# Batch 0's keys and queries loaded in turn by head pair, and 2 KB rows for the keys and queries of batches 2 and 3

## The chip, the cores and the metric

The kernel runs on one core of a Trainium2 chip. The metric is the device time of one execution in microseconds (us), lower is better. The core has a matrix engine (TensorE, PE in the profile, with its weight loads as PEld), a vector engine (VectorE, DVE), an activation engine (ScalarE, ACT), a general engine (GpSimd, POOL) and a sync engine (SyncE, SP) which issues transfers. Each engine works through its own queue in order. Matrix results go to PSUM, everything else lies in SBUF, both of 128 partitions.

## The reference

```python
batch, n_heads, seq, head_dim = (4, 8, 768, 64)      # q, k, v
block, window = (32, 16)
k_sum = k.reshape(B, H, nb, block, D).max(axis=3)    # nb = 24 blocks
v_sum = v.reshape(B, H, nb, block, D).mean(axis=3)
scores_l = scale * q @ k.T, kept where abs(i - j) < window
scores_s = scale * q @ k_sum.T + log(block)
a = softmax(concat(scores_l, scores_s))
attn = a @ concat(v, v_sum)
x = attn as [3072 tokens, 512]
h = x @ w_in                                          # [512, 2048]
out = (h * sigmoid(beta * h)) @ w_out                 # [2048, 512]
```

So each query attends to the keys less than 16 places away and to 24 block summaries (maximum of the keys, mean of the values), and the result goes through two products with a gated activation between them.

## The kernel before

The four batches run one after the other. A batch has eight heads, held as four pairs g = 0 to 3: the 64 dimensions of one head in partitions 0 to 63, of the other in 64 to 127. Queries are cut in 12 tiles of 64 (QT). For a tile the 96 keys of its window and the 24 block keys make up to 120 rows of a score tile; a score group is half of a pair's tiles (u = 0 or 1). An exp on ACT (`weigh`, L316) turns a group into weights `e`, and PE multiplies them with the values `ve` (for even tiles) and `vo` (the same values shifted by 64 rows, for odd tiles).

**The head** (L111 to L614) computes attention of batch 0 while its inputs arrive. Everything there is in an order written by hand, and each engine's queue follows it. `sw_load` (L84, issued by POOL) loads rows of 8 consecutive tokens, 2 KB of f32 to a packet, and casts them to bf16 in `krow` and `qrow`; it loads four pairs of keys in four transfers (L122 to L147), then queries 0, 1, and 2 and 3 together (L163 to L165). `turned` (L248) lets PE turn such rows into PSUM, 16 matmuls for a pair; `kt0` (L259) copies the keys to `kT` and may take their block maximum `km` (`key_max_nat`), and `qt_pe` (L272) copies the queries to `qn`. `scores0` (L282) makes a score group straight from `kT`, `km` and `qn`, with masks as extra matmuls (`off`, `edge`). `vm0` averages the values into `vm_one`, `av_split` weighs the values for u = 0, `norm` divides by the sum, `x_pe` turns the result into `xT`. `blank_run` issues matmuls on zeros that nothing uses. The matmuls `begin` (L602) start the first product with `w_in`.

The loads that follow in POOL's queue are four parts of `w_in` (`load_w_in`; the first waits on an exp by `behind`, L578), `w_out` in four parts, and between them `krow` and `qrow` of batch 1 as one transfer each (`more_loads`, L629). SP loads the values: batch 0's pairs 1 to 3 wait until the first query load has landed (L167), batch 1's until the last part of `w_out` has (L639). Batch 1's keys and queries are turned on PE as batch 0's are (`kt_pe`, `qt_pe`).

**Batches 2 and 3** take another way. `hw_load` (L87, issued by SP) loads a pair as 128-row blocks of f32, 256 bytes to a packet, into a staging tile; POOL casts it (`kq_cast`, L453) into a tile of the pool `nat`; a transposing DMA (`kq_dma`, L465) writes `kT` and `qn`; DVE copies the windows of 96 keys (`windows_nat`, L225) and takes the block maximum. This happens while PE runs the first product of the batch before (`h_tile`, L490). The second product (`o_atom`, L513) is interleaved with the scores of the next batch (`scores`, L302), whose moving operand is `q_tile` (L279), 64 consecutive elements of `qn`.

`run` (L530) puts the work of such a stage in order: a list of main steps, and side steps with a position among them, sorted.

Of the kernel before, what the change touches and what calls it, by code (L numbers as in the profile page):

```python
# [11 lines left out]
def kernel(  # L12
# [29 lines left out]
    G = H // 2  # L42
    NK = QT + 2 * W
    CS = (8, 8)
    scale = 1.0 / math.sqrt(D)
    log_block = math.log(block)
    d_model = moe_w_in.shape[0]
# [6 lines left out]

    const = ctx.enter_context(tc.tile_pool(name="consts", bufs=1))
    stage = ctx.enter_context(tc.tile_pool(name="stage", bufs=4))
    natp = ctx.enter_context(tc.tile_pool(name="nat", bufs=4))
    ep = ctx.enter_context(tc.tile_pool(name="ep", bufs=8))
    xp = ctx.enter_context(tc.tile_pool(name="xp", bufs=4))
    op = ctx.enter_context(tc.tile_pool(name="op", bufs=3))  # L60
# [7 lines left out]
    def pair(a, b, g):  # L68
        return a[b, 2 * g:2 * g + 2]
# [14 lines left out]
    def sw_load(t, src, b, lo, hi):  # L84
        return nc.gpsimd.dma_start(out=row_view(t, b, lo, hi), in_=src[b, lo:hi].rearrange("h (p c) d -> p h (c d)", c=CS[b]))

    def hw_load(nm, src, b, g):  # L87
        f = stage.tile([P, 2, J6, D], f32, name=nm + "st", tag=nm + "st")
        stg[(nm, b, g)] = f
        nc.sync.dma_start(out=f[:], in_=pair(src, b, g).rearrange("h (j p) d -> p h j d", p=P))  # L90

    vst = [const.tile([P, JV, D], f32, name=f"vst{g}") for g in range(G)]

# [28 lines left out]
    sw_load(krow, k, 0, 0, 2)  # L122
    identity = const.tile([P, P], bf16, name="identity")
    make_identity(nc, identity)
    sw_load(krow, k, 0, 2, 4)
    band = const.tile([P, QT], bf16, name="band")
    mask = const.tile([P, NT, QT], bf16, name="mask")
    off = const.tile([P, NK + QT], bf16, name="off")
# [14 lines left out]
    nc.vector.memset(A, 0.0)  # L143
    As = A[:, :, 0:nb]
    nc.vector.memset(As, 1.0 / block)
    sw_load(krow, k, 0, 4, 6)
    sw_load(krow, k, 0, 6, 8)  # L147
    select(off[:], -1, [[1, NK + QT]], -1, NEG)
    select(off[:], 2 * W - 1, [[-1, NK + QT]], 1, NEG)
    identity32 = const.tile([P, P], f32, name="identity32")  # L150
# [9 lines left out]
    nc.vector.memset(vm_one[NK:NK + nb, :, :, D:VW], 1.0)  # L160
    for t in (ve, vo):
        nc.vector.memset(t[:, :, :, D:VW], 1.0)
    ql = sw_load(qrow, q, 0, 0, 2)  # L163
    sw_load(qrow, q, 0, 2, 4)
    qe = sw_load(qrow, q, 0, 4, 8)  # L165
    vl = [None] + [load_v0(g) for g in range(1, G)]
    behind(vl[1], ql)  # L167
    select(band[:], -1, [[-1, QT]], 1)
    select(band[:], 2 * W - 1, [[1, QT]], -1)
    select(As, -W, [[P, J6 + 1], [-block, nb]], 1)  # L170
    select(As, block - 1 + W, [[-P, J6 + 1], [block, nb]], -1)

    def more_masks():
        nc.vector.tensor_copy(out=mask[:], in_=band[:, None, :].to_broadcast([P, NT, QT]))
        nc.vector.memset(mask[0:W, 0], 0.0)
        nc.vector.memset(mask[NK:NK + nb], 1.0)

    def clear_kw():
        for g in range(G):
# [36 lines left out]
    def windows_perm(cp, g, src, C):  # L216
# [4 lines left out]
        e = kw[g][:, 0, W:NK]  # L221
        cp(strided(e, [[(NT - 1) * P - W, 2], [C, F + FW], [1, C]]),
           strided(src[:, :, 0:1], [[R - F - FW, 2], [1, F + FW], [cs, C]]))

    def windows_nat(cp, g):  # L225
        cp(kw[g][:, :, 0:NK], strided(kT[g][:, 0:1], [[QT, NT], [1, NK]]))

    def key_max_win(g):
        nc.vector.tensor_reduce(out=km[g][:, NK:NK + nb].rearrange("p (m n) -> p m n", n=2),  # L229
# [46 lines left out]

    et = {}

    def q_tile(g, h, m):  # L279
        return qn[g][h * D:(h + 1) * D, m * QT:(m + 1) * QT]  # L280

    def scores0(g, u, bg, pe=True):  # L282
        s = big[bg]
# [18 lines left out]
    def scores(b, g, u, bg):  # L302
        s = big[bg]
        for j in range(HT):
            m = u * HT + j
            for h in range(2):
                nc.tensor.matmul(s[:, h, j * QT:(j + 1) * QT], kw[g][h * D:(h + 1) * D, m, :], q_tile(g, h, m),  # L307
                                 start=True, stop=True)
        weigh(b, g, u, s)
        if g < G - 1 or b == 1:  # L310
            mask_e(b, g, u)
# [136 lines left out]
                                    in_=xn[(b, g)].rearrange("p j h d -> p (j h d)"))  # L448


    nat = {}

    def kq_cast(eng, nm, b, g):  # L453
        t = natp.tile([P, J6, 2, D], bf16, name=nm + "n", tag=nm + "n")
        nat[(nm, b, g)] = t
        return eng.tensor_copy(out=t[:], in_=stg[(nm, b, g)].rearrange("p h j d -> p j h d"))  # L456

    last_mask = {}

    def key_cast(n, g):  # L460
        i = kq_cast(nc.gpsimd, "k", n, g)
        if g == 0 and n - 1 in last_mask:
            behind(i, last_mask[n - 1])

    def kq_dma(nm, b, g):  # L465
        t = kT[g][:, W:W + S] if nm == "k" else qn[g][:]
        nc.sync.dma_start_transpose(out=t.rearrange("p (j t) -> p j t", j=J6),
                                    in_=nat[(nm, b, g)].rearrange("p j h d -> p (j h d)"))


    def h_begin(i, t, lo, hi):
# [70 lines left out]

    blank_run(30)
    load_beta()
    blank_run(32, QT)
    kt0(0, 0, act_cp)
    more_masks()
    blank_run(12, QT)
    kt0(1, 1, act_cp, False)
    blank_run(8)  # L550
    kt0(2, 2, dve_cp, False)
    key_max_nat(1)
    blank_run(10)
    kt0(3, 0, act_cp, False)
    blank_run(4)
    v_cast(nc.gpsimd, 0)
    v_odd(nc.gpsimd, 0, 0, 3)
    v_odd(nc.gpsimd, 0, 3, 6)
    select(mask[0:NK, NT - 1], QT + W - 1, [[0, QT]], -1)

    def av0(g, t):
        av_split(g, t[:, 0])
        norm(0, g, t, [0])

    qt_pe(0, 0, 1, act_cp)
    vm0(0, one[0], dve_cp)
    blank_run(9)
    vm_rest(nc.gpsimd, 0)
    qt_pe(0, 1, 2, dve_cp)
    scores0(0, 0, 0)  # L570
    scores0(1, 0, 1)
    key_max_nat(2)
    key_max_nat(3)
    we = scores0(0, 1, 2)
    av0(0, one[1])
    scores0(1, 1, 0)
    qt_pe(0, 2, 1, dve_cp)
    behind(load_w_in(0, 512), we)  # L578
    v_cast(nc.gpsimd, 1)
    x_pe(0, 0, 0, dve_cp, one[0])  # L580
    qt_pe(0, 3, 2, act_cp)
    scores0(2, 0, 0)
    v_odd(nc.gpsimd, 1, 0, 3)
    v_cast(nc.vector, 2)
    v_odd(nc.vector, 2, 0, 3)
    scores0(3, 0, 1)
    scores0(2, 1, 2, False)
    vm0s(1, 2, one[1], dve_cp)
    scores0(3, 1, 0, False)
    load_w_in(512, 1024)  # L590
    v_cast(nc.gpsimd, 3)
    av0(1, one[0])
    av_two(0, 1, [big[2][:, 0:1]])
    v_odd(nc.gpsimd, 3, 0, 3)
    vm0(3, big[1][:, 1:2], dve_cp)
    av0(2, one[1])
    x_pe(0, 1, 0, act_cp, one[0])
    av0(3, big[1][:, 0:1])
    load_w_in(1024, 1536)
    load_w_in(1536, 2048)  # L600

# [1 line left out]
        for i in (2 * p, 2 * p + 1):  # L603
            h_begin(i, big[(2, 0, 1)[p % 3]][:, i % 2], lo, hi)

    begin(0, 0, 1)
    begin(1, 0, 1)
    x_pe(0, 2, 0, act_cp, one[1])
    silu_table()
    begin(0, 1, 2)  # L610
    begin(1, 1, 2)
    x_pe(0, 3, 0, dve_cp, one[0])
    begin(0, 2, 3)
    begin(1, 2, 3)  # L614
# [45 lines left out]

    def load_keys(n):
        for g in range(G):
            hw_load("k", k, n, g)


    def scores_at(b, s, pos):
# [41 lines left out]
    for b in range(1, B):  # L708
        n = b + 1
        s = []  # L710
        if n < B:
            for g in range(2):
                s.append((0 + .1 * g, lambda g=g, n=n: hw_load("q", q, n, g)))
            for g in range(G):
                s.append((.5 + g, lambda g=g: key_cast(n, g)))
                s.append((.6 + g, lambda g=g: kq_dma("k", n, g)))
                s.append((3.5 + g, lambda g=g: windows_nat(dve_cp, g)))
                s.append((3.6 + g, lambda g=g: key_max_nat(g)))
                s.append((4.7 + g, lambda g=g: kq_cast(nc.gpsimd, "q", n, g)))
                s.append((8 + g, lambda g=g: key_sums(nc.gpsimd, g)))  # L720
                s.append((6.6 + 1.5 * g, lambda g=g: kq_dma("q", n, g)))
                s.append((12.6 + 1.2 * g, lambda g=g: v_cast(nc.gpsimd, g)))
                s.append((12.7 + 1.2 * g, lambda g=g: v_odd_dma(g)))
            for g in range(2):
                s.append((.7 + g, lambda g=g, n=n: hw_load("q", q, n, g + 2)))
                s.append((2.7 + g, lambda g=g: load_v(n, g)))
                s.append((6.7 + 1.5 * g, lambda g=g: load_v(n, g + 2)))
        if n + 1 < B:
            for g in range(G):
                s.append(((16.31, 16.32, 19.3, 19.31)[g], lambda g=g, n=n: hw_load("k", k, n + 1, g)))  # L730
        late = [x for x in s if x[0] >= 16]
        run([lambda i=i: h_tile(i) for i in range(k2)], [x for x in s if x[0] < 16])
        s = [((x[0] - 16) * 1.2, x[1]) for x in late]
        if n < B:
            scores_at(n, s, [1, 5.9, 8, 10.1])
            av_at(n, s, [10.2, 13.1, 13.2, 13.3], [0, 1, 2, 0])
            for g in range(G):
                s.append(((10.3, 13.35, 13.4, 13.5)[g], lambda g=g: x_dma(n, g)))
            s.append((5.99, lambda: vm_all(big[0], VMC)))
            s.append((6.3, lambda: spread(0)))  # L740
            s.append((8.3, lambda: spread(1)))
        main = [lambda ms=ms, a=a: o_atom(b, ms, a) for ms in range(J6 - (n == B)) for a in range(4)]
        run(main, s)
        if n == B:
            ms = J6 - 1
            for lo, hi in ((0, 256), (256, 512)):
                t = one[0 if lo else 1][:, 0]
                for kk in range(k2):
                    o_mm(ms, kk, t, lo, hi)
                o = op.tile([P, hi - lo], f32, name="o_half", tag=f"o_half{lo}", bufs=1)  # L750
                nc.vector.tensor_copy(out=o[:], in_=t[:, 0:hi - lo])
                nc.sync.dma_start(out=out_r[b * J6 + ms][:, lo:hi], in_=o[:])
# [29 lines left out]
```

## Time and profile before

| | |
|---|---|
| median of three runs | 216.02 us (215.3 to 217.65) |
| the profiled execution | 217.07 us, its span 215.33 us |
| PE clock granted in the span | 1.00 |
| HBM read, written | 27.37 MB, 6.29 MB |
| DMA packets | 85,287, of which 73,728 under 512 B |

A line of the chain of waits gives start, length and what ran; the chain is followed back from the last instruction to whatever released it. A row of the lines' view gives source line, engine, operation, output<-input with shapes, count, then busy time in us and mean ns of one, then idle time of the engine before them and what ended it. In the windows' view each row is a stretch of the span with the busy time of PE, PEld, DVE, ACT and POOL, the granted clock, the DMA share and GB/s. Rows of the timeline give start, length, engine, line, operation, and in brackets the idle time ahead.

Where the time lies: 0 to 25 us is the head; to 50 us the first product of batch 0 (with the last part of its attention in it); to 78 us its second product and batch 1's attention; then 46 us for each of batches 1 and 2 with the attention of the next one, and 45 us for batch 3.

### The profile page before, as it was taken

The page shows a single profiled execution, that of the slowest core. Times are in us where ns is not written, and L with a number is a line of the kernel's source. Part 1 is how long each engine was busy: PE and PEld are TensorE (multiplying, and loading weights), DVE is VectorE, ACT ScalarE, POOL GpSimd, SP SyncE. Part 2 cuts the span into 40 slices and gives each one's busy share as a digit, 9 for nine tenths or more (in the row PEclk, how much of TensorE's full clock was granted, in tenths as well). Part 3 has the DMA queues.
Part 4 walks back from the last instruction along what each step waited for, and adds up shares of the span by engine and source line. Part 5 has one row for each costly group of instructions (what it writes and reads, how often), then busy time and mean ns, then how long its engine had stood idle before and what let it go on. Part 6 is the DMA issues. An engine that isn't in the chain of part 4 may idle for free.

```text
span 215.3 us, 5346 instructions
## 1 busy us (share of the span) xinstructions
PE 207.2 (96%) x2242; PEld 121.0 (56%) x2242; DVE 99.1 (46%) x233; ACT 107.7 (50%) x143; POOL 57.5 (27%) x91
## 2 busy tenths in 40 slices
PE   7789999999999999999999999999999999999993
PEld 7567756665546445665455455654564556654452
DVE  5567766597786612530599212422796200002121
ACT  2258595777676007776681046676660077650000
POOL 7946990010517403441105004433000000000000
PEclk9999999999999999999999999999999999999999
DMA  6999999999949999999699979999527400001212
GB/s 118 181 212 161 191 175 198 206 209 191 225 114 226 269 199 236 230 195 159 147 215 214 247 184 227 180 200 196 136 70 182 120 24 0 0 3 49 97 49 97
DMA packets 85287, 34.09 MB, mean 158 GB/s; under 512 B 73728, under 2 KB 82320, under 8 KB 85264
## 3 DMA queue, kind: packets, MB, share of 16 engines
q1 hardware_dynamic: 68192, 24.05, 55.3%
q0 software_dynamic: 7440, 7.34, 21.3%
q10 hardware_dynamic: 9632, 2.37, 7.6%
q8 instruction: 17, 0.28, 0.6%
q14 instruction: 6, 0.05, 0.1%
HBM read 27.37 MB, written 6.29 MB: 156 GB/s over the span
## 4 chain that ended last, share of the span: by engine, by line
PE 87%; DMA 6%; DVE 3%; issue 1%; ACT 0%; POOL 0%; POOLq 0%; DVEq 0%
PE one L505 36%; PE big L487 29%; PE big L473 5%; PE one L479 3%; DMA xT<-xn 3%; DMA krow<-in_k_dram 3%; PE big L256 3%; PE big L307 3%; PE big L395 2%; PE big L479 2%; DVE xn L422 1%; DVE qn L243 1%; PE big L294 1%; PE big L286 1%; PE big L369 1%
## 5 line engine op out<-in xcount | busy, mean ns | idle before, releaser
L505 PE MATMUL one<-w_out_sb,h_sb 128*128 128x512 bf16 (+1 forms) x400 | 86.3, 371 | 0.0
L500 ACT ACTIVATE h_sb<-big,beta_sb 128x768 bf16<-128x768 f32 x48 | 42.7, 901 | 52.5 <-PE big L487 52.5
L487 PE MATMUL big<-xT,w_in_sb 128*128 128x384 bf16 x384 | 63.0, 326 | 0.3 <-DMA xT<-xn 0.3
L505 PEld LDWEIGHTS <-h_sb 128*128 128x128 bf16 x400 | 37.8, 98 | 40.9 <-issue 0.2
L487 PEld LDWEIGHTS <-w_in_sb 128*128 128x128 bf16 x384 | 37.6, 98 | 25.6 <-issue 0.5
L243 DVE COPY o_sb<-one 128x512 f32<-128x512 f32 x20 | 13.8, 688 | 47.4 <-PE one L505 47.3
L316 ACT ACTIVATE e<-big,bias 128x768 bf16<-128x768 f32 x32 | 27.1, 899 | 7.5 <-PE big L307 4.9
L320 DVE TENSOR_TENSOR e<-e,mask 128x768 bf16<-128x768 bf16 x24 | 14.2, 618 | 19.0 <-ACT e L316 18.9
L325 POOL CAST ve<-vst 128x832 bf16<-128x832 f32 x15 | 13.2, 889 | 9.8 <-DMA vst<-in_v_dram 9.7
L243 DVE COPY kw<-kT 128x1152 bf16<-128x1152 bf16 x8 | 4.0, 496 | 22.5 <-DMA kT<-kn 22.5
L456 POOL CAST qn<-qst 128x768 bf16<-128x768 f32 x8 | 6.6, 830 | 28.7 <-DMA qst<-in_q_dram 28.7
L237 POOL COPY kw<-km 128x288 bf16<-128x288 bf16 x12 | 5.5, 471 | 27.6 <-DVE km L229 21.7
L422 DVE TENSOR_TENSOR xn<-big,r 128x768 bf16<-128x768 f32 (+1 forms) x14 | 12.6, 900 | 0.5
L233 DVE TENSOR_REDUCE km<-kT 128x24 bf16<-128x768 bf16 x12 | 11.2, 943 | 2.4 <-ACT kT L240 2.4
L473 PE MATMUL big<-xT,w_in_sb 128*128 128x384 bf16 x64 | 11.4, 326 | 0.0
L456 POOL CAST kn<-kst 128x768 bf16<-128x768 f32 x8 | 6.5, 828 | 13.8 <-DVE e L320 11.4
L620 ACT ACTIVATE h_sb<-big,beta_sb 128x384 bf16<-128x384 f32 x16 | 8.1, 580 | 2.7 <-PE big L473 2.7
L522 PE MATMUL one<-blank 128*128 128x128 bf16 (+1 forms) x105 | 7.2, 231 | 1.3 <-DVE blank L118 1.3
L479 PEld LDWEIGHTS <-w_in_sb 128*128 128x128 bf16 x64 | 6.1, 98 | 4.0
L479 PE MATMUL one<-xT,w_in_sb 128*128 128x384 bf16 x44 | 8.1, 326 | 0.0
L473 PEld LDWEIGHTS <-w_in_sb 128*128 128x128 bf16 x64 | 5.9, 98 | 3.5
L395 PEld LDWEIGHTS <-e 128*64 128x64 bf16 x336 | 6.2, 111 | 2.1 <-issue 1.6
(122 smaller groups left out, 187.8 us busy)
## 6 DMA issues: line engine op xcount, KB each, us to landing
out_dram<-o_sb SPq DMA_DIRECT2D x23, 256.0 KB, 2.5
vst<-in_v_dram SPq DMA_DIRECT2D x13, 336.0 KB, 4.6
kst<-in_k_dram SPq DMA_DIRECT2D x8, 384.0 KB, 5.4
qst<-in_q_dram SPq DMA_DIRECT2D x8, 384.0 KB, 4.1
w_in_sb<-in_moe_w_in_dram POOLq DMA_DIRECT2D x4, 512.0 KB, 6.1
w_out_sb<-in_moe_w_out_dram POOLq DMA_DIRECT2D x4, 512.0 KB, 14.2
vo<-ve SPq DMA_DIRECT2D x12, 107.2 KB, 2.3
vst<-in_v_dram SPq DMA_DIRECT2D x3, 416.0 KB, 6.8
```

The lines of the kernel that those rows point to most:

```text
L233: nc.vector.tensor_reduce(out=km[g][:, NK:NK + nb], in_=kT[g][:, W:W + S].rearrange("p (n f) -> p n f", f=block), op=ALU.max, axis=AX.X)
L243: nc.vector.tensor_copy(out=o, in_=i)
L316: return nc.scalar.activation(out=e[:], in_=s[:, :, 0:HS], func=ACTF.Exp, bias=bias[:, 0:1], scale=scale)
L320: return (nc.gpsimd if (b, g) == (1, G - 1) else nc.vector).tensor_mul(out=e.rearrange("p h (m q) -> p h m q", q=QT), in0=e.rearrange("p h ...
L325: eng.tensor_copy(out=ve[:, g, lo:hi, 0:D], in_=vst[g][:, lo:hi])
L422: nc.vector.tensor_mul(out=x[:, 3 * us[0]:3 * us[0] + 3 * n].rearrange("p (k j) h d -> p k (j h) d", k=n), in0=tv[:, :, :, 0:D], in1=r[:, ...
L456: return eng.tensor_copy(out=t[:], in_=stg[(nm, b, g)].rearrange("p h j d -> p j h d"))
L473: nc.tensor.matmul(t[:, 0:HS], w_in_sb[:, ki, i * P:(i + 1) * P], xT[:, ki, 0:HS], start=(ki == 0), stop=(ki == k1 - 1))
L479: nc.tensor.matmul(t[:, 0:HS], w_in_sb[:, ki, i * P:(i + 1) * P], xT[:, ki, lo:lo + HS], start=(ki == 0), stop=(ki == k1 - 1))
L487: nc.tensor.matmul(t[:, kk, 0:HS], w_in_sb[:, ki, i * P:(i + 1) * P], xT[:, ki, kk * HS:(kk + 1) * HS], start=(ki == 0), stop=(ki == k1 - 1))
L500: nc.scalar.activation(out=h_sb[:, i, :].rearrange("p (k m) -> p k m", k=2), in_=t[:, :, 0:HS], func=ACTF.Silu, scale=beta_sb[:, i:i + 1])
L505: nc.tensor.matmul(t[:, 0:hi - lo], h_sb[:, n, ms * P:(ms + 1) * P], w_out_sb[:, n, lo:hi], start=(n == 0), stop=(n == k2 - 1))
```

## The change

It has two parts.

*The head.* The loads of batch 0 alternate: keys of pair 0, queries of pair 0, keys of pair 1, and so on, eight transfers of one pair each. SP's loads of v's pairs 1 to 3 now wait on the keys of pair 2 (the fifth load) instead of the queries of pair 0 (the fifth load before). The scores of a pair are placed as its keys and queries land. The masks move from DVE to POOL, some copies change between ACT and DVE, the number of blank matmuls goes from 105 to 82, and the first `w_in` load no longer waits on an exp, but stands behind the cast of v's pair 1.

*Batches 2 and 3.* `row_load` takes 8 consecutive tokens to a row, 2 KB to a packet, in 96 partitions. The casts write into `krow` and `qrow` instead of the pool `nat`, and those of keys of pairs 1 and 3 are done by DVE. The transposing DMA turns eight blocks of 96 rows instead of six of 128, so tokens lie in `kT` and `qn` with a step of 96 elements between neighbours. For the keys, the window copies put them in order (`windows_perm`, two copies for a pair), and the block maximum is taken from the windows. For the queries, `q_tile` reads `qn` with that step as the matmul's moving operand.

```diff
+    CK = 8
+    RK = S // CK
...
-    natp = ctx.enter_context(tc.tile_pool(name="nat", bufs=4))
...
-    def hw_load(nm, src, b, g):
-        f = stage.tile([P, 2, J6, D], f32, name=nm + "st", tag=nm + "st")
+    def row_load(nm, src, b, g):
+        f = stage.tile([RK, 2, CK * D], f32, name=nm + "st", tag=nm + "st")
         stg[(nm, b, g)] = f
-        nc.sync.dma_start(out=f[:], in_=pair(src, b, g).rearrange("h (j p) d -> p h j d", p=P))
+        nc.sync.dma_start(out=f[:], in_=pair(src, b, g).rearrange("h (p c) d -> p h (c d)", c=CK))
...
     make_identity(nc, identity)
+    sw_load(qrow, q, 0, 0, 2)
     sw_load(krow, k, 0, 2, 4)
+    sw_load(qrow, q, 0, 2, 4)
...
-    sw_load(krow, k, 0, 4, 6)
+    kl = sw_load(krow, k, 0, 4, 6)
+    sw_load(qrow, q, 0, 4, 6)
     sw_load(krow, k, 0, 6, 8)
+    sw_load(qrow, q, 0, 6, 8)
...
-    ql = sw_load(qrow, q, 0, 0, 2)
-    sw_load(qrow, q, 0, 2, 4)
-    qe = sw_load(qrow, q, 0, 4, 8)
     vl = [None] + [load_v0(g) for g in range(1, G)]
-    behind(vl[1], ql)
+    behind(vl[1], kl)
...
     def more_masks():
-        nc.vector.tensor_copy(out=mask[:], in_=band[:, None, :].to_broadcast([P, NT, QT]))
+        nc.gpsimd.tensor_copy(out=mask[:], in_=band[:, None, :].to_broadcast([P, NT, QT]))
...
+    def q_tile(g, h, m, b=0):
+        r = slice(h * D, (h + 1) * D)
+        if b < 2:
+            return qn[g][r, m * QT:(m + 1) * QT]
+        F = QT // CK
+        return strided(qn[g][r, m * F:m * F + 1], [[1, F], [RK, CK]])
...
+    def nat_view(nm, g):
+        return {"k": krow, "q": qrow}[nm][0:RK, g * CK * 2 * D:(g + 1) * CK * 2 * D]
 
     def kq_cast(eng, nm, b, g):
-        t = natp.tile([P, J6, 2, D], bf16, name=nm + "n", tag=nm + "n")
-        nat[(nm, b, g)] = t
-        return eng.tensor_copy(out=t[:], in_=stg[(nm, b, g)].rearrange("p h j d -> p j h d"))
+        t = nat_view(nm, g).rearrange("p (c h d) -> p c h d", c=CK, h=2)
+        return eng.tensor_copy(out=t, in_=stg[(nm, b, g)].rearrange("p h (c d) -> p c h d", c=CK))
...
+    KC = [nc.gpsimd, nc.vector, nc.gpsimd, nc.vector]
...
-        i = kq_cast(nc.gpsimd, "k", n, g)
+        i = kq_cast(KC[g], "k", n, g)
...
-        t = kT[g][:, W:W + S] if nm == "k" else qn[g][:]
-        nc.sync.dma_start_transpose(out=t.rearrange("p (j t) -> p j t", j=J6),
-                                    in_=nat[(nm, b, g)].rearrange("p j h d -> p (j h d)"))
+        t = kT[g][:, 0:S] if nm == "k" else qn[g][:]
+        nc.sync.dma_start_transpose(out=t.rearrange("p (j t) -> p j t", j=CK),
+                                    in_=nat_view(nm, g))
...
-                s.append((3.5 + g, lambda g=g: windows_nat(dve_cp, g)))
-                s.append((3.6 + g, lambda g=g: key_max_nat(g)))
+                s.append((3.5 + g, lambda g=g: windows_perm(dve_cp, g, kT[g][:, 0:S].rearrange("p (c r) -> p c r", c=CK), CK)))
+                s.append((3.6 + g, lambda g=g: key_max_win(g)))
```

The head's order after the change, whose lines replace L543 to L614 (the `begin` calls behind it take two parts of xT at once for pairs 0 and 1):

```python
blank_run(30); load_beta(); blank_run(28, QT)
kt0(0, 0, act_cp); blank_run(8, QT)
qt_pe(0, 0, 1, act_cp); blank_run(8)
kt0(1, 2, act_cp)
v_cast(nc.gpsimd, 0); v_odd(nc.gpsimd, 0, 0, 3)
scores0(0, 0, 0); scores0(0, 1, 1)
v_odd(nc.gpsimd, 0, 3, 6); more_masks()
qt_pe(0, 1, 2, dve_cp); kt0(2, 0, act_cp, False)
vm0(0, one[0], dve_cp)
scores0(1, 0, 1); scores0(1, 1, 2)
vm_rest(nc.gpsimd, 0); key_max_nat(2)
av_split(0, one[1][:, 0])
qt_pe(0, 2, 0, dve_cp); norm(0, 0, one[1], [0])
kt0(3, 1, act_cp)
v_cast(nc.gpsimd, 1); load_w_in(0, 512)
scores0(2, 0, 2); qt_pe(0, 3, 0, dve_cp); scores0(2, 1, 1, False)
v_odd(nc.vector, 1, 0, 3); x_pe(0, 0, 0, act_cp, one[0]); blank_run(8)
scores0(3, 0, 0); vm0(1, one[1], dve_cp); scores0(3, 1, 2, False)
v_cast(nc.gpsimd, 2); load_w_in(512, 1024); v_cast(nc.gpsimd, 3)
av_split(1, one[0][:, 0]); v_odd(nc.vector, 2, 0, 3); norm(0, 1, one[0], [0])
vm0(2, one[1], act_cp); v_odd(nc.vector, 3, 0, 3); av0(2, big[1][:, 0:1])
x_pe(0, 1, 0, act_cp, one[0]); vm0(3, one[1], act_cp); silu_table()
av_two(0, 1, [big[0][:, 0:1]]); av0(3, one[0])
load_w_in(1024, 1536); load_w_in(1536, 2048)
```

More of the change, by code (lines that the diff above doesn't have):

```diff
@@ L173, in more_masks @@
     def more_masks():
-        nc.vector.tensor_copy(out=mask[:], in_=band[:, None, :].to_broadcast([P, NT, QT]))
-        nc.vector.memset(mask[0:W, 0], 0.0)
-        nc.vector.memset(mask[NK:NK + nb], 1.0)
+        nc.gpsimd.tensor_copy(out=mask[:], in_=band[:, None, :].to_broadcast([P, NT, QT]))
+        nc.gpsimd.memset(mask[0:W, 0], 0.0)
+        nc.gpsimd.memset(mask[NK:NK + nb], 1.0)
+        select(mask[0:NK, NT - 1], QT + W - 1, [[0, QT]], -1)
     def clear_kw():
@@ L223, in windows_perm @@
            strided(src[:, :, 0:1], [[R - F - FW, 2], [1, F + FW], [cs, C]]))
-    def windows_nat(cp, g):
-        cp(kw[g][:, :, 0:NK], strided(kT[g][:, 0:1], [[QT, NT], [1, NK]]))
     def key_max_win(g):
@@ L277 @@
     et = {}
-    def q_tile(g, h, m):
-        return qn[g][h * D:(h + 1) * D, m * QT:(m + 1) * QT]
+    def q_tile(g, h, m, b=0):
[4 more added lines that the diff above has]
+        return strided(qn[g][r, m * F:m * F + 1], [[1, F], [RK, CK]])
     def scores0(g, u, bg, pe=True):
@@ L306, in scores @@
             for h in range(2):
-                nc.tensor.matmul(s[:, h, j * QT:(j + 1) * QT], kw[g][h * D:(h + 1) * D, m, :], q_tile(g, h, m),
+                nc.tensor.matmul(s[:, h, j * QT:(j + 1) * QT], kw[g][h * D:(h + 1) * D, m, :], q_tile(g, h, m, b),
                                  start=True, stop=True)
@@ L448, in x_dma @@
                                     in_=xn[(b, g)].rearrange("p j h d -> p (j h d)"))
-    nat = {}
+    def nat_view(nm, g):
+        return {"k": krow, "q": qrow}[nm][0:RK, g * CK * 2 * D:(g + 1) * CK * 2 * D]
     def kq_cast(eng, nm, b, g):
-        t = natp.tile([P, J6, 2, D], bf16, name=nm + "n", tag=nm + "n")
-        nat[(nm, b, g)] = t
-        return eng.tensor_copy(out=t[:], in_=stg[(nm, b, g)].rearrange("p h j d -> p j h d"))
+        t = nat_view(nm, g).rearrange("p (c h d) -> p c h d", c=CK, h=2)
+        return eng.tensor_copy(out=t, in_=stg[(nm, b, g)].rearrange("p h (c d) -> p c h d", c=CK))
     last_mask = {}
+    KC = [nc.gpsimd, nc.vector, nc.gpsimd, nc.vector]
     def key_cast(n, g):
-        i = kq_cast(nc.gpsimd, "k", n, g)
+        i = kq_cast(KC[g], "k", n, g)
         if g == 0 and n - 1 in last_mask:
@@ L544 @@
     load_beta()
[L545 to L559, printed above, removed]
+    blank_run(28, QT)
     def av0(g, t):
@@ L563, in av0 @@
         norm(0, g, t, [0])
+    kt0(0, 0, act_cp)
+    blank_run(8, QT)
     qt_pe(0, 0, 1, act_cp)
+    blank_run(8)
+    kt0(1, 2, act_cp)
+    v_cast(nc.gpsimd, 0)
+    v_odd(nc.gpsimd, 0, 0, 3)
+    scores0(0, 0, 0)
+    scores0(0, 1, 1)
+    v_odd(nc.gpsimd, 0, 3, 6)
+    more_masks()
+    qt_pe(0, 1, 2, dve_cp)
+    kt0(2, 0, act_cp, False)
     vm0(0, one[0], dve_cp)
-    blank_run(9)
+    scores0(1, 0, 1)
+    scores0(1, 1, 2)
     vm_rest(nc.gpsimd, 0)
-    qt_pe(0, 1, 2, dve_cp)
-    scores0(0, 0, 0)
-    scores0(1, 0, 1)
     key_max_nat(2)
[L573 to L578, printed above, removed]
-    v_cast(nc.gpsimd, 1)
[L580 to L589, printed above, removed]
+    av_split(0, one[1][:, 0])
+    qt_pe(0, 2, 0, dve_cp)
+    norm(0, 0, one[1], [0])
+    kt0(3, 1, act_cp)
+    v_cast(nc.gpsimd, 1)
+    load_w_in(0, 512)
+    scores0(2, 0, 2)
+    qt_pe(0, 3, 0, dve_cp)
+    scores0(2, 1, 1, False)
+    v_odd(nc.vector, 1, 0, 3)
+    x_pe(0, 0, 0, act_cp, one[0])
+    blank_run(8)
+    scores0(3, 0, 0)
+    vm0(1, one[1], dve_cp)
+    scores0(3, 1, 2, False)
+    v_cast(nc.gpsimd, 2)
     load_w_in(512, 1024)
     v_cast(nc.gpsimd, 3)
[L592 to L596, printed above, removed]
+    av_split(1, one[0][:, 0])
+    v_odd(nc.vector, 2, 0, 3)
+    norm(0, 1, one[0], [0])
+    vm0(2, one[1], act_cp)
+    v_odd(nc.vector, 3, 0, 3)
+    av0(2, big[1][:, 0:1])
     x_pe(0, 1, 0, act_cp, one[0])
-    av0(3, big[1][:, 0:1])
+    vm0(3, one[1], act_cp)
+    silu_table()
+    av_two(0, 1, [big[0][:, 0:1]])
+    av0(3, one[0])
     load_w_in(1024, 1536)
@@ L604, in begin @@
             h_begin(i, big[(2, 0, 1)[p % 3]][:, i % 2], lo, hi)
[L606 to L611, printed above, removed]
+    begin(0, 0, 2)
+    x_pe(0, 2, 0, dve_cp, one[1])
+    begin(1, 0, 2)
     x_pe(0, 3, 0, dve_cp, one[0])
@@ L662, in load_keys @@
         for g in range(G):
-            hw_load("k", k, n, g)
+            row_load("k", k, n, g)
     def scores_at(b, s, pos):
@@ L712 @@
             for g in range(2):
-                s.append((0 + .1 * g, lambda g=g, n=n: hw_load("q", q, n, g)))
+                s.append((0 + .1 * g, lambda g=g, n=n: row_load("q", q, n, g)))
             for g in range(G):
@@ L724 @@
             for g in range(2):
-                s.append((.7 + g, lambda g=g, n=n: hw_load("q", q, n, g + 2)))
+                s.append((.7 + g, lambda g=g, n=n: row_load("q", q, n, g + 2)))
                 s.append((2.7 + g, lambda g=g: load_v(n, g)))
@@ L729 @@
             for g in range(G):
-                s.append(((16.31, 16.32, 19.3, 19.31)[g], lambda g=g, n=n: hw_load("k", k, n + 1, g)))
+                s.append(((16.31, 16.32, 19.3, 19.31)[g], lambda g=g, n=n: row_load("k", k, n + 1, g)))
         late = [x for x in s if x[0] >= 16]
```

## The prediction

> **What bounds the kernel now.** I read the busy line first, then busy time by stage, then the chain of waits in order of time, then the rows of the DMA issues and of single lines.
>
> The page:
> ```profile
> span 215.3 us, 5346 instructions
> PE 207.2 (96%) x2242; PEld 121.0 (56%) x2242; DVE 99.1 (46%) x233; ACT 107.7 (50%) x143; POOL 57.5 (27%) x91
> ```
> By stage (start:end, length, busy time per engine, granted clock, DMA share, GB/s):
> ```profile
> 6.00:11.70 5.70, 4.06 (x98) 3.22 (x98) 3.99 (x6) 2.40 (x3) 5.35 (x11) 1.00 1.21 185
> 11.70:19.20 7.50, 6.75 (x175) 5.57 (x177) 4.80 (x9) 4.68 (x6) 2.75 (x6) 1.00 0.99 197
> 19.20:25.30 6.10, 5.88 (x155) 4.88 (x156) 4.64 (x13) 4.17 (x6) 5.74 (x11) 1.00 1.15 176
> 25.30:50.10 24.80, 24.78 (x248) 15.42 (x248) 17.81 (x53) 18.44 (x34) 7.88 (x13) 1.00 1.19 197
> 50.10:78.20 28.10, 27.72 (x382) 14.30 (x382) 18.41 (x36) 13.90 (x20) 10.71 (x12) 1.00 1.04 203
> ```
> From 25.3 us on PE is full, at clock 1.00; between there and the last matmul it is idle for 0.4 us. So time can come only from the head (PE idles 1.3 us at the start and 2.9 us from 1.3 to 25.3, and fills 7.2 us with blank matmuls, L522), from that 0.4 us, or from dearer PE work. The chain:
> ```profile
> 18.15 0.97 DVE qn L243
> ...
> 25.30 0.76 PE big L473 x4
> ...
> 27.04 5.23 PE big L473 x32
> ...
> 40.46 0.80 PE big L256 x32
> ...
> 60.86 0.51 PE big L369 x28
> ...
> 71.43 6.74 DMA xT<-xn
> 78.17 0.04 issue
> ```
> The queries of heads 4 and 5 are copied at 18.15 to 19.12, and four of the eight score groups (L286 to L299) come behind that. The uninterrupted first product starts at 27.04.
>
> **The head, part by part.** The eight loads of batch 0 land in this trace at 6.0, 7.1, 9.1 and 10.1 (keys), 11.6 and 12.4 (queries 0, 1) and 14.6 (queries 2, 3 in one load), each 192 KB written. I keep these eight times as slots and give them to the new order: k0 6.0, q0 7.05, k1 9.1, q1 10.1, k2 11.4, q2 12.4, k3 13.4, q3 14.6. POOL issues seven of them in a row from 2.73 (0.65 us each); the select on `off`, which stood between them, now ends at 8.0.
>
> Durations: 16 turning matmuls 0.49; a copy out of PSUM 0.80 on ACT, 0.96 on DVE; key maximum 0.94; a score group 0.60, without the mask matmuls 0.44; exp 0.84; `vm0` 0.50 and its copy 0.30; `av_split` 0.60; a norm 0.75; turning x 0.17. In queue order, 0.04 us per handover:
> - k0 at 6.01, q0 at 7.09, k1 9.14 to 9.63. kT0 and qn0 are copied by 8.42, its maximum by 8.32, so the first two score groups run 9.63 to 10.83 (before: from 13.74, under a DVE copy).
> - q1 to 11.32, k2 11.44 to 11.93, `vm0` to 12.43. qn1 on DVE ends 12.41, behind km1. Scores of g1 to 13.65, av of g0 to 14.25, q2 to 14.74, k3 to 15.23.
> - qn2 stands behind km2 and av: 14.78 to 15.74. Scores g2 from 15.78, q3 16.38 to 16.87. qn3 stands behind norm and km3: 17.43 to 18.39. So g3's scores start at 18.43, PE having waited 0.5 us for each of qn2 and qn3.
> - The rest: scores, `vm0`s, av's, x turns, with one wait of 0.34 us for ACT's copy of vm_one: `begin` at 23.62, the first product uninterrupted from 25.26.
>
> 27.04 - 25.26 = **1.78 us** for PE alone. ACT and POOL cover what they get: the masks move from DVE to POOL (0.54 + 0.70 us there, about 1.9 on POOL by its 0.83 for 768 elements), and POOL is then free at 15.4, ahead of v's second load at 16.3. Without that cover every us would delay w_in.
>
> **What takes part of it back.** From 20 us to 50 us the DMA engines are full, and this stream doesn't follow PE:
> ```profile
> 17.68 0.76 POOL L203 DMA_DIRECT2D w_in_sb<-in_moe_w_in_dram  x1 [3.58 <-ACT e L316]
> ...
> 28.68 0.80 POOL L85 DMA_DIRECT2D krow<-in_k_dram  x1
> ```
> ```profile
> krow<-in_k_dram POOLq DMA_DIRECT2D x1, 768.0 KB, 11.2
> ```
> w_in lands at 23.2, 26.6, 29.2, 32.1, w_out's first part at 36.0, batch 1's keys at 28.68 + 11.2 = 39.9, and PE turns them at 40.46: 0.5 us of slack. Batch 1's v waits behind w_out's last part (48.0); the last cast of it ends on POOL at 59.59 + 0.88 = 60.47, and PE takes it at 60.86: 0.39 us of slack. The change drops the wait of the first w_in load on exp, but puts it behind the cast of v's second load (landed 16.3), so it is issued at about 17.23, 0.45 us earlier. The head can thus hand on 0.45 + 0.39 = 0.84 us (0.95 at the keys); the remainder becomes PE waiting for krow at 39 and for ve at 60. I take **0.8 us**; its ends are 0 (stream not earlier, slack eaten by v's order) and 1.78 (stream keeps up).
>
> **Batches 2 and 3.** Keys and queries come as 2 KB rows instead of 256 B: 24,576 packets become 3,072. PE waits for DMA only at 78.17 (0.3 us, xT); with lighter key loads just ahead of that I take **0.3 us** of gain, bounds 0 and 0.4. Four key casts go from POOL (0.83 each) to DVE (1.01 for 832 elements, so about 1.24), and the windows become two strided copies. These rows bound them:
> ```profile
> L243 DVE CAST kw<-big 128x960 bf16<-128x960 f32 x4 | 4.6, 1148 | 2.5 <-PE big L256 2.5
> L243 DVE COPY kw<-kT 128x1152 bf16<-128x1152 bf16 x8 | 4.0, 496 | 22.5 <-DMA kT<-kn 22.5
> L307 PE MATMUL big<-qn,kw 64*128 64x64 bf16 x288 | 6.3, 191 | 0.0
> ```
> 1.15 + 0.31 instead of 0.50: DVE gets about 6.5 us more per stage of 20.8 us in which it is busy 5.65 us. The first windows stand ready about 8 us before the scores at 100.5 need them, the fourth 14 us before. On DVE the third key cast stands behind windows that wait for kT, and the fourth transpose on SP waits for it: still ahead of its old 89.3. All of it costs nothing; with the cover gone it would be some 4 us a batch.
>
> Not covered is `q_tile`: the moving operand of 192 score matmuls now steps 192 B between elements. No matmul of this trace does that. Twelve pairs of L307 take 0.46 us (38 ns a pair); a pair of L286, of 384 columns, takes 160 ns, so 64 columns take 27 ns and a pair isn't bound by them. Lower end 0 us (a gain is excluded: work is the same). Upper end: half rate and halves of a pair no longer beside each other, 107 instead of 38 ns, 96 x 69 = 6.6 us. Nearest is the strided read that the trace has: the CAST above reads PSUM at steps of 512 B, and its 960 elements take 190 ns more than the 768 of the `qn` copy, 1.0 ns per element as in any f32 copy there. So I take 0.
>
> [...]
>
> **Sum.** -0.8 - 0.3 = -1.1 us. The profiled run took 217.07 us (span 215.33), 1.05 above the median of 216.02; on the median: **214.9 us**. About 1% (2.2 us) is what a measurement here can tell from no change.
>
> **Rivals.**
> - *The stream keeps up.* If w_in comes out earlier than I have it (v's second load rides on k2, whose slot may be earlier) and the slots of q0 to q3 move up, the whole 1.78 + 0.3 arrives, 213.9, and up to 1.9 us of my remaining waits with it: 212.0 to 213.9. For: POOL issues the loads without the select. Against: the DMA share of 1.15 to 1.21 in the head.
> - *Strided q at half rate.* A pair goes from 38 to 53 ns, or gains the full 27: 96 x 15 to 27 = 1.5 to 2.6 us: 216.3 to 217.5.
> - *Strided q serialises the pair*: 6.6 us, 221.5, slower. It decides from (218.2 - 214.9) / 96 = 34 ns more per pair. For: nothing hides PE time after 25 us. Against: the strided PSUM reads above.
>
> **Chances.** Forecast 0.35 (214.0 to 215.8). Stream keeps up 0.33, of which 0.30 over 1%. Half rate 0.15, all within 1%. Serialised 0.17. So faster 0.30, same 0.35 + 0.03 + 0.15 = 0.53, slower 0.17. The range leaves out the serialised case (0.17) and the last of the second (0.03): 212.6 to 218.0.
>
> **What would show it.** First-product stretch from about 25.3 instead of 27.0; PE idle of about 0.8 us before batch 1's keys near 39 or before L369's counterpart near 60; no xT wait at 77; 24 strided score matmuls in 0.46 us (0.64 to 0.78 at half rate, 1.3 serialised). The prediction is wrong if w_in is issued after 17.7, if k1 lands past 10, or if PE waits for kw in batch 2.

## The result and the profile after

The changed kernel takes 223.21 us (median of four executions, 222.66 to 226.18) against 216.25 us (four, 215.3 to 217.65): 1.0315 times as long, 95% interval 1.0279 to 1.0352, so about 6.8 us slower. The profiled execution is the longest of the four (226.18 us): the clock granted to PE was 0.50 in it from about 16 to 22 us, so the ratio leaves it out, and the head is read from another run below.

The page of the changed kernel, its clock row with one digit for each fortieth of the span:
```profile
span 224.4 us, 5300 instructions
PE 215.4 (96%) x2203; PEld 129.5 (58%) x2219; DVE 106.9 (48%) x243; ACT 108.3 (48%) x145; POOL 60.8 (27%) x88
...
PEclk9995999999999999999999999999999999999999
...
L311 PE MATMUL big<-qn,kw 64*128 64x64 bf16 x288 | 14.0, 252 | 0.1
```
PE is still full, with 39 fewer matmuls recorded and 8.2 us more busy time. (23 of the 39 are blank matmuls; the other 16 are missing from the trace, which has 384 of the 400 of L510.) The last row names the place: the score matmuls took 6.3 us before (191 ns mean, the row of L307 in the prediction) and now take 14.0 (252 ns mean), with the same count. Nothing waits more there (0.1 us of idle time). The chain of waits shows the 24 score matmuls of a pair of heads, forecast at 0.46 us:
```profile
79.49 20.80 PE big L492 x128
...
102.02 1.41 PE big L311 x24
...
106.99 1.41 PE big L311 x24
...
111.61 1.41 PE big L311 x24
...
114.86 1.41 PE big L311 x24
```
Instead of 0.46 us each takes 1.41. With four pairs in each of two batches that is 8 x 0.95 = 7.6 us, all on the path, because PE has no idle time for it (the 0.1 us of that row).

What the change put on other engines came about as costed or cheaper (rows by line and shape):
```profile
L243 DVE COPY kw<-kT 128x960 bf16<-128x960 bf16 x8 | 8.6, 1077 | 12.2 <-DMA kT<-krow 12.2
L243 DVE COPY kw<-kT 128x160 bf16<-128x160 bf16 x8 | 3.1, 384 | 0.0
L460 DVE CAST krow<-kst 96x1024 bf16<-96x1024 f32 x4 | 2.7, 686 | 0.0
```
The windows take 1.08 + 0.38 us a pair (1.15 + 0.31 estimated) and a key cast on DVE 0.69 (1.24 estimated).

### The profile page after: what moved, and what is told of

It is laid out like the page before. It is cut to its first block, busy times and chain, and to the rows that moved or that the text cites. A ratio compares the mean times of both kernels' runs of the same rounds, so it can differ in the third digit from the quotient of the medians.

```text
span 224.4 us, 5300 instructions
## 1 busy us (share of the span) xinstructions
PE 215.4 (96%) x2203; PEld 129.5 (58%) x2219; DVE 106.9 (48%) x243; ACT 108.3 (48%) x145; POOL 60.8 (27%) x88
## 4 chain that ended last, share of the span: by engine, by line
PE 90%; issue 3%; DMA 2%; DVE 2%; POOL 1%; ACT 1%; DVEq 0%; POOLq 0%
PE one L510 36%; PE big L492 28%; PE big L311 6%; PE big L478 5%; PE one L484 3%; PE big L256 2%; DMA qrow<-in_q_dram 2%; PE big L399 2%; PE big L484 1%; POOL e L324 1%; PE big L298 1%; PE big L290 1%; DVE qn L243 1%; PE one L345 1%; PE big L373 1%
## 5 line engine op out<-in xcount | busy, mean ns | idle before, releaser
L510 PE MATMUL one<-w_out_sb,h_sb 128*128 128x512 bf16 (+1 forms) x384 | 83.8, 370 | 1.8 <-issue 1.4
L510 PEld LDWEIGHTS <-h_sb 128*128 128x128 bf16 x400 | 37.8, 98 | 41.5 <-issue 1.1
L324 DVE TENSOR_TENSOR e<-e,mask 128x768 bf16<-128x768 bf16 x24 | 13.4, 571 | 23.8 <-ACT e L320 23.7
L460 POOL CAST qrow<-qst 96x1024 bf16<-96x1024 f32 x8 | 8.8, 1097 | 30.1 <-DMA qst<-in_q_dram 28.7
L243 DVE COPY kw<-kT 128x960 bf16<-128x960 bf16 (+1 forms) x16 | 11.0, 730 | 12.2 <-DMA kT<-krow 12.2
L329 POOL CAST ve<-vst 128x832 bf16<-128x832 f32 x16 | 14.5, 923 | 7.3 <-DMA vst<-in_v_dram 5.2
L237 POOL COPY kw<-km 128x288 bf16<-128x288 bf16 x12 | 7.7, 646 | 32.0 <-DVE km L229 29.9
L311 PE MATMUL big<-qn,kw 64*128 64x64 bf16 x288 | 14.0, 252 | 0.1
L311 PEld LDWEIGHTS <-kw 64*128 64x128 bf16 x288 | 11.3, 104 | 4.4 <-issue 4.2
L229 DVE TENSOR_REDUCE km<-kw 128x24 bf16<-128x768 bf16 x12 | 11.3, 949 | 0.2
L460 POOL CAST krow<-kst 96x1024 bf16<-96x1024 f32 x4 | 4.1, 1036 | 15.1 <-DVE e L324 14.9
```

Source lines behind the costliest of these rows:

```text
L243: nc.vector.tensor_copy(out=o, in_=i)
L324: return (nc.gpsimd if (b, g) == (1, G - 1) else nc.vector).tensor_mul(out=e.rearrange("p h (m q) -> p h m q", q=QT), in0=e.rearrange("p h ...
L329: eng.tensor_copy(out=ve[:, g, lo:hi, 0:D], in_=vst[g][:, lo:hi])
L460: return eng.tensor_copy(out=t, in_=stg[(nm, b, g)].rearrange("p h (c d) -> p c h d", c=CK))
L510: nc.tensor.matmul(t[:, 0:hi - lo], h_sb[:, n, ms * P:(ms + 1) * P], w_out_sb[:, n, lo:hi], start=(n == 0), stop=(n == k2 - 1))
```

## The experiments

The theory: the strided operand of the score matmuls costs 7.6 us, and the head gives back under 1. Its rivals: the new loads, casts and copies of batches 2 and 3 cost time as well, or the head itself lost some. All ratios are to the kernel before, run on the same chip, with their 95% interval in brackets.

**The two parts alone.** The first run has before's head and all of the change in batches 2 and 3. The second has the change's head and before's batches. The first in part, against the change; the second makes the reverse of these edits in the kernel before:

```diff
-    kl = sw_load(krow, k, 0, 4, 6)
-    sw_load(qrow, q, 0, 4, 6)
+    sw_load(krow, k, 0, 4, 6)
...
-    behind(vl[1], kl)
+    behind(vl[1], ql)
```

> Head of before, batches 2 and 3 as in the change. Theory 1 (the 192 B step of q in the score matmuls is the whole loss): a strided group of 24 matmuls takes 1.41 us instead of 0.46 as in the profile after, 8 x 0.95 = 7.6 us, so 223 to 224 us, start of the uninterrupted first product at 27.0 as before. Theory 2 (the loss is in the head, whose clock fell to half in the profile after): within 1 us of before, 215 to 217.

> Head of the change, batches 2 and 3 as in before. Theory 1: the head gains what the change lacks to 7.6 us, about 0.7 us, so 215.0 to 216.0; the L307 groups take 0.46 us. Theory 2: 3 us or more slower, 219 and up, with a PE gap of 0.9 us and a lower granted clock in the head. If transfers cap the head's gain as the prediction has it, the first product starts 1.5 us or more earlier and PE then waits about 0.8 us for the turning of batch 1's keys or for the averages of batch 1's values.

Measured: batches alone 223.53 us, 1.0352 (1.0318 to 1.0387), +7.6 us; head alone 215.94, 1.0013 (0.9982 to 1.0044). The whole loss is in batches 2 and 3, and the head is worth nothing that can be measured. The chain of the run with the batches alone:
```profile
26.30 5.23 PE big L476 x32
...
55.54 0.46 PE big L309 x24
...
99.36 1.42 PE big L309 x24
```
The same line takes 0.46 us in batch 1, whose queries lie side by side, and 1.42 in batch 2. This kernel has before's head, and its first product starts at 26.30, not at the 27.04 from which the prediction counted. The chains of two later runs, the patterns and the halves below, have that head as well:
```profile
25.87 5.23 PE big L479 x32
```
```profile
26.13 5.23 PE big L480 x32
```

The chain of the run with the head alone:
```profile
12.97 0.61 issue
13.58 0.39 PE big L296 x9
...
25.11 0.43 issue
25.54 0.37 DVE xT L245
25.95 5.36 PE big L475 x32
...
39.50 0.80 PE big L258 x32
...
59.90 0.51 PE big L371 x28
```
The first product starts at 25.95, inside the range of the four traces with before's head (25.87 to 27.04). PE loses 0.61 us to "issue" at 12.97, in the middle of a score group. The 0.84 us from 25.11 to 25.95, in which the chain follows a copy into `xT`, isn't a loss of that size: PE runs four matmuls of the second pair and the turning of x meanwhile (its timeline has them from 24.88 and 25.53), and is late by at most 0.25 us. There is no wait for `krow` at 39.5 or for `ve` at 59.9. The keys were issued at 25.9 and took 11.9:
```profile
L85 POOL DMA_DIRECT2D krow<-in_k_dram x5: 632/639/821, 1.4 to 25.9; - x5
```
so they landed at 37.8, 1.7 us before PE wanted them. Neither of these two runs waits for xT near 77.

**The order of the queries put right, by two engines, and before's way.** The third run lets the transposing DMA write a tile `qp` and DVE put it in order, reading neighbours and writing every eighth element; the fourth takes before's way for the queries alone (packets of 256 bytes) and keeps the rest of the change; a later one gives the copies to POOL, which reads 192 B apart and writes neighbours, and puts them earlier in the order of the stage:

```diff
+    def q_order(g):
+        nc.vector.tensor_copy(out=qn[g].rearrange("p (f c) -> p c f", c=CK), in_=qp[g].rearrange("p (c f) -> p c f", c=CK))
...
-        nc.vector.tensor_copy(out=qn[g].rearrange("p (f c) -> p c f", c=CK), in_=qp[g].rearrange("p (c f) -> p c f", c=CK))
+        nc.gpsimd.tensor_copy(out=qn[g].rearrange("p (f c) -> p f c", c=CK), in_=qp[g].rearrange("p (c f) -> p f c", c=CK))
...
-                s.append(((14.5, 15.5, 18, 20)[g], lambda g=g: q_order(g)))
+                s.append(((13, 15.2, 16.5, 17.5)[g], lambda g=g: q_order(g)))
```

> The whole change, but DVE copies batch 2's and 3's queries into order before the scores read them (8 copies, about 1 us each, beside PE's work). Theory 1: 24 score matmuls take 0.46 us again, 214.5 to 215.7 us, 0.5 to 1.5 us under before. Theory 2: no change against the kernel after, 222 to 224. If the casts, window copies and 2 KB rows cost time of their own, it stays over 217.

> The whole change, but the queries of batches 2 and 3 come by the way of before (256 B packets, natural order), so no score matmul steps. Theory 1 (only the step and DVE's late ordering copies cost): 215 to 216.5, as the head alone (215.94). Rival (2 KB rows, DVE casts or strided window copies cost by themselves): over 217.

> As the kernel with DVE's ordering copies, but POOL makes them, reading in steps of 192 B and writing neighbours (there: reading neighbours, writing in steps of 16 B, 1.8 to 1.9 us a copy). Theory 1: about 1 us a copy, nothing of DVE's or PE's waits for it but the scores: 215 to 216.5. Rival (the ordering itself is too late for the scores whoever makes it): PE waits for qn in batches 2 and 3, 218 or more.

Measured: DVE's copies 220.35 us, 1.0206 (1.0148 to 1.0263); before's way 216.14, 1.0005 (0.9967 to 1.0044); POOL's copies 216.32, 1.0016 (0.9986 to 1.0047). In all three the score matmuls are back at 191 ns in the mean. So with the queries as before, all else that the change does in batches 2 and 3 costs nothing that can be measured: its casts, windows and masks are hidden, and so are POOL's copies. DVE's are not. Its row, its chain, and PE's wait in that run (us in all, times, longest), then POOL's row:
```profile
L460 DVE COPY qn<-qp 128x768 bf16<-128x768 bf16 x8 | 15.8, 1978 | 3.9 <-DMA qp<-qrow 3.9
```
```profile
103.31 1.90 DVE qn L460
105.21 0.50 DVE o_sb L244
105.71 1.79 DVE qn L460
```
```profile
PE big L308 <- ACT e L317: 3.2, 4, 1.2
```
```profile
L460 POOL COPY qn<-qp 128x768 bf16<-128x768 bf16 x8 | 12.5, 1575 | 0.9 <-DMA qp<-qrow 0.9
```
A copy that writes every eighth element takes 1978 ns, where a window copy that reads 192 B apart takes 1077 for more elements. It stands in DVE's queue ahead of other copies (`o_sb`, which frees PSUM, and `vm_sb`), and the score matmuls come to wait 3.2 us in four waits for ACT's exps, whose chain leads back to these DVE copies. That was a fault of this experiment, not of the change. POOL's version differs in the engine, the order of reading and the place among the side steps; which of them made the difference was not taken apart.

**The step moved from the read to the write.** Reading runs of 8 neighbours and writing PSUM in the order of the tokens:

```diff
-        return strided(qn[g][r, m * F:m * F + 1], [[1, F], [RK, CK]])
+        return strided(qn[g][r, m * F:m * F + 1], [[RK, CK], [1, F]])
...
+                    o = o.rearrange("p (f c) -> p c f", c=CK)
```

> The whole change, but a score matmul reads runs of 8 neighbouring elements (192 B apart) and its write into PSUM puts them in order (32 B between neighbours). If only 16-byte lines of SBUF cost: 24 matmuls take 0.46 us, 215 to 216.5. If steps cost in PSUM as in SBUF: 1.4 us, 222 to 224.

Measured: 218.7 us, 1.0119 (1.0071 to 1.0168), with one line of its chain:
```profile
102.75 0.78 PE big L314 x24
```
It is better than the change and worse than before: 8 x 0.32 = 2.6 us, which is what the whole kernel lost (1.2%). Since the same reads alone cost nothing in the next run, this is the price of writing f32 at steps of 32 B.

**What in the step costs.** Before's kernel with another pattern of 64 elements for each pair of batches 2 and 3, one execution (219.43 us):

```diff
+    PAT = {(2, 0): [[2, 64]], (2, 1): [[4, 64]], (2, 2): [[8, 64]], (2, 3): [[12, 64]],
+           (3, 0): [[1, 8], [96, 8]], (3, 1): [[96, 8], [1, 8]], (3, 2): [[24, 32], [1, 2]], (3, 3): [[48, 16], [1, 4]]}
```

> The kernel before, with other columns of qn read by the score matmuls of batches 2 and 3 (other queries, so another output), one pattern for each pair: batch 2: steps of 4, 8, 16 and 24 B; batch 3: 8 elements 192 B apart eight times over (as in the change), runs of 8 elements 192 B apart, pairs of elements 48 B apart, runs of 4 elements 96 B apart. If a new 16-byte line for each element is what costs: 24 matmuls take 0.46 us for steps of 4 and 8 B and for runs of 8, 4 and 2, and 1.41 us for steps of 16, 24 and 192 B. If any step other than one element costs: 1.41 us for all steps, less for the runs. If the cost grows with the distance: 16 and 24 B well below 1.41.

Its chain:
```profile
99.12 0.46 PE big L313 x24
...
103.14 0.81 PE big L313 x24
...
107.16 1.48 PE big L313 x24
...
110.47 1.48 PE big L313 x24
...
147.67 1.42 PE big L313 x24
...
152.65 0.46 PE big L313 x24
...
156.31 0.80 PE big L313 x24
...
158.95 0.58 PE big L313 x24
```
In the order of the patterns: steps of 4, 8, 16 and 24 B, the change's own (192 B), runs of eight, runs of two 48 B apart, runs of four 96 B apart. Neither distance nor being strided as such decides: runs of 16 B that lie 192 B apart cost nothing (0.46 us), while 16 B steps cost as much as 192 B ones (1.48 and 1.42). What fits is how many of the elements lie together in 16 B: four or more are free or nearly so (0.46 to 0.58), two cost 1.7 times, one 3.1 to 3.2 times. No view names what lies behind the 16 B.

An estimate of mine from these rows is that a read costs nothing as long as it is shorter than the 38 ns which a pair takes anyway: 64 pieces of 16 B in 118 to 123 ns and 32 in 67 are about 2 ns a piece; 16 would then take some 32 ns and stay under the 38. The runs of four, with 48 ns, don't fit this, and a matmul with a lower floor was not measured.

**Whether the halves of a pair still run side by side.** Before's kernel with single pairs changed, one execution (219.56 us): one head alone, stepped or not, one head stepped and the other not, and all matmuls of one head issued ahead of the other's:

```diff
+        if (b, g) in ((2, 0), (2, 1), (3, 0)) and (h == 0 or (b, g) != (2, 0)):
+            return strided(qn[g][r, m * 8:m * 8 + 1], [[1, 8], [96, 8]])
...
+        if (b, g) in ((2, 1), (2, 2)):
+            jh = [(j, h) for h in range(2) for j in range(HT)]
+        if (b, g) in ((3, 0), (3, 1)):
+            jh = jh[0::2]
```

> The kernel before; score matmuls of batches 2 and 3 read or run otherwise (other output; groups (3,0) and (3,1) leave out the second head of a pair): (2,0) first head in steps of 192 B, second in neighbours; (2,1) both in steps, all six of one head, then of the other; (2,2) as (2,1) without steps; (3,0) first head alone, in steps; (3,1) first head alone, neighbours. If the two heads' stepped reads run one after the other: (2,0) about 0.8 us for 24, (3,0) 0.7 for 12. If they run side by side, each at a quarter of the rate: (2,0) near 1.4, (3,0) near 1.4 for 12.

Its chain, first the stepped head alone, then the head alone with neighbours:
```profile
148.26 1.41 PE big L314 x12
...
153.23 0.45 PE big L314 x12
```
Twelve stepped matmuls of one head take 1.41 us, as the 24 of both do: 118 ns each, so the second head is free beside the first. (With neighbours one head alone takes 0.45, 38 ns each.) The timeline, by which 24 matmuls of neighbours take 0.52 us, has 1.48 us where one head is stepped and the other is not, and 1.69 where both are and one head's matmuls are issued ahead of the other's; one by one, 24 stepped matmuls of 118 ns would take 2.8.

**The gap in PE's instructions.** In the change's head PE stops in the middle of a group, waiting for nothing on record. The timeline of the run with the head alone:
```profile
12.73 0.23 PE L296 MATMUL big<-qn,kT 64*96 64x64 bf16 x3
...
13.58 0.41 PE L296 MATMUL big<-qn,kT 64*96 64x64 bf16 x9 [0.61 <-issue]
```
Two runs take blank matmuls out of this head: two short runs of them (32 PE instructions with their weight loads), then 82 narrow ones replaced by 17 of 512 columns (130 instructions fewer, 118 of them ahead of the interrupted score group):

```diff
     kt0(0, 0, act_cp)
-    blank_run(8, QT)
     qt_pe(0, 0, 1, act_cp)
-    blank_run(8)
...
-    blank_run(30)
+    blank_run(8, 512)
```

> Head of the change without its two short runs of blank matmuls (16 matmuls and weight loads fewer ahead of the scores of heads 2 and 3), batches 2 and 3 as in before. The head alone has a PE gap of 0.6 us after the 3rd of 12 window matmuls of score group (1,1), at which nothing shown is awaited. If it is instruction loading, the gap sits 32 instructions later in the program (in the av matmuls behind that group) or is gone; if it is a wait of that score group, it stays there.

> Head of the change with 17 blank matmuls of 512 columns in place of 82 of 64 or 128 (130 PE instructions fewer ahead of the scores), batches 2 and 3 as in before. If the PE gap is the loading of the instructions behind the 446th, PE comes to that place only after 15 us and the gap is gone: first product about 0.5 us earlier than in the head alone (25.95), time 215.0 to 215.6. If the gap is no instruction loading, or if transfers cap the head, no change: 215.9.

Measured: 216.17 us, 1.0008 (0.9972 to 1.0044), and 215.51 us, 0.9970 (0.9943 to 0.9997). The timelines, one after the other:
```profile
13.11 0.33 PE L405 MATMUL one<-vm_one,e 128*128 128x65 bf16 x5
13.64 0.20 PE L405 MATMUL one<-vm_one,e 128*128 128x65 bf16 x1 [0.20 <-issue]
```
```profile
14.11 0.46 PE L258 MATMUL big<-identity,krow 96*64 96x96 bf16 x14
14.95 0.23 PE L258 MATMUL big<-identity,krow 96*64 96x96 bf16 x2 [0.38 <-issue]
```
In all three the gap comes after the same number of recorded PE instructions, 446 (223 weight loads and 223 matmuls), whatever the next one does. A packet on the instruction queue (17 packets with 0.28 MB on the page of before, so 16 KB each) starts at 11.0 to 11.5 us in the first two and 12.5 to 13.0 in the third; the gap ends 2.0 to 2.6 us later. From these times I guess that PE waits for its own program; no view names that wait, which is 0.20 to 0.61 us in these heads. I had expected the gap to vanish with wide blanks, and it did not: fewer instructions bring PE to the place at 14.57, but the packet starts later too. In the kernel before the packet starts at 9.0 to 9.5, and PE gets there near 14 without a gap. Why it starts later with the new head was not found.

The version with wide blanks is the only one of nine whose interval lies below 1, by a hair (0.3% faster than before); with so many versions compared, that is no shown gain over before. It is faster than the change. Its chain:
```profile
25.53 1.15 PE big L475 x6
26.73 0.46 issue
27.18 2.47 ACT h_sb L618 x5
29.67 1.47 PE big L475 x8
```
PE starts the first product at 25.53. The chain then passes through ACT, which empties PSUM, but PE loses little there: its 32 matmuls take 5.61 us by the timeline, where the head alone has 5.36. One more run added four matmuls of the first product (`begin(2, 0, 2)`) where the chain passes through the copy into `xT`:

> As the kernel with wide blanks, and four matmuls of the third pair of first-product tiles (begin(2, 0, 2)) run while DVE still copies xT of heads 6 and 7, where the head alone waits 0.84 us (25.11 to 25.95). If that wait is on the path: 0.5 to 0.65 us less, 214.4 to 215.0, faster than before and than the change. If something later (transfers, batch 1's values) sets the time: no change against the wide blanks.

Measured: 216.36 us, 1.0000 (0.9976 to 1.0024). Nothing came of it, and its chain shows one reason:
```profile
19.08 6.99 DMA w_in_sb<-in_moe_w_in_dram
26.07 0.05 issue
26.11 1.81 PE big L475 x10
```
The added matmuls need the second part of `w_in`, and PE idles 0.49 us for it. It lands at 26.07: here the transfers do hold PE back. And there was little to fill, since PE had been at work for most of the 0.84 us that the run was to use.

## Why the prediction was wrong, point by point

**The step that failed** is the price of `q_tile`: "Nearest is the strided read that the trace has: the CAST above reads PSUM at steps of 512 B ... So I take 0." It was 0.95 us for each 24 matmuls, 7.6 us in all, above even the upper end of 6.6. The cast was no near row: it is another engine reading another memory, at 1.0 ns an element, where PE's 27 ns for 64 columns are 0.42 ns a column. That the slower reader keeps its pace says nothing of the faster one. The argument that a pair "isn't bound" by its 64 columns held for steps of 4 B (0.46 us for 24) and no longer for 8 B (0.81). The strided rivals had the right sign, with 0.32 of the chance between them.

**The rivals.** "Strided q serialises the pair" forecast 1.3 us for 24 matmuls and 221.5 us; it was 1.41 and 223.2. Its sign was right; that its size came near was luck, because its mechanism was wrong: a pair went from 38 to 118 ns, and one head alone takes the same 118. The halves stay side by side, each at about a third of its rate (38 to 118 ns). "Half rate", an assumption that no row of before shows, is what a step of 8 B would have cost (0.81 against 0.64 to 0.78 forecast). That the stream of transfers keeps up is true of the keys of batch 1 (no wait at 39.5), but it brought nothing.

**The head**, forecast at a gain of 0.8 us out of 1.78, gained nothing that can be measured: alone it took 0.3 us more than before (between 0.4 less and 0.95 more). About half of the 1.78 was in its base. The 27.04 is the latest of four traces with before's head; the other three start the first product at 25.87 to 26.30, which takes 0.7 to 1.2 us away. PE's schedule for the new head, 25.26, came out nearly right but for one wait that no row of before shows: 25.95 measured, of which 0.61 us are the gap in PE's instructions. In other traces of this head that gap was 0.23 us (queries by before's way, first product at 25.70) and 0.87 (DVE's copies, 26.26). The cap by the transfers was not reached at batch 1's keys: with the first `w_in` load issued at 16.8 (16.7 with the old head in the first run), they were issued at 25.9 instead of 27.7, and `krow` came 1.7 us ahead of need. It was there in another place: in the last run PE stood waiting for the second part of `w_in` at 26.1.

**The 0.3 us of xT wait** did not come back as a gain that can be counted. PE waits for xT there in two of the seven traces with before's key loads (0.30 us before, 0.57 in the run of the halves) and in none of the six with the lighter ones. Whether the lighter loads remove it, or it comes and goes by itself, so few traces can't tell.

**What was costed at nothing and hidden** held: casts on DVE, windows, masks on POOL. With only the queries' way put back the time was before's within 0.45%.

## What to carry to other kernels

The moving operand of a 64-column bf16 matmul cost nothing here in runs of 16 B (0.46 us for 24, as with neighbours) and took 1.41 us in single elements 192 B apart; if a cheaper load leaves it in another order, put the order right in a copy that some idle engine does (here POOL, 1575 ns a copy, at no cost that could be measured), not in PE's read, when PE is the bound. A price taken from another engine and another memory is no bound: where the trace has no like row, the expensive end deserves the larger chance, and one kernel with a few patterns measures it. A gain of under 1 us in a head should be counted from several traces, since the same head ended anywhere from 25.87 to 27.04 us. And a wait on the chain is lost time for PE only if PE is idle in it, which its timeline tells.

## What the runs showed of the hardware that was not expected

- Score matmuls with a moving operand of 64 bf16 columns took 38 ns for a pair of heads at steps of 4 B, 67 at 8 B, 123 at 16 and 24 B, and 118 at 192 B.
- The write has its own price: the score matmuls that wrote f32 to PSUM at steps of 32 B took 1.7 times as long (0.78 us instead of 0.46 for 24).
- A DVE copy that steps 16 B in the write took 1978 ns for 768 elements, one that steps 192 B in the read 1077 for 960; POOL took 1575 for 768 with the latter.
- "Issue" time of PE stood at a fixed place in its program, after 446 recorded instructions, in three heads, whatever was scheduled there (0.20, 0.38 and 0.61 us). That it is the loading of its instructions is a guess from the packet that starts 2.0 to 2.6 us before the gap's end; no view shows it.
